# Linear attention with a gated MoE: queries projected with the tokens moving, the row maximum taken across partitions, three quads of keys unpaired

## The chip, the core and the metric

The kernel runs on one core of a Trainium2 chip. The metric is the device time of one launch in microseconds (us), the median of three runs. Engines are named as in the profile: PE is TensorE (matmuls; PEld its weight loads), DVE is VectorE, ACT is ScalarE, POOL is GpSimd, SP is SyncE, whose queue issues the DMAs.

## The reference

Eight batches, eight heads, 576 tokens, head dimension 64. Queries and keys go through the same feature map with 128 features: a projection, minus the largest absolute value of each row, then exp of it and of its negative.

```
def phi(x):
    proj = np.einsum('bhsd,df->bhsf', x, w_phi)
    proj = proj - np.max(np.abs(proj), axis=-1, keepdims=True)
    return np.concatenate([np.exp(proj), np.exp(-proj)], axis=-1)
q_p, k_p = (phi(q), phi(k))
kv = np.einsum('bhsf,bhsd->bhfd', k_p, v)
z = np.sum(k_p, axis=2)
num = np.einsum('bhsf,bhfd->bhsd', q_p, kv)
den = np.einsum('bhsf,bhf->bhs', q_p, z)[..., None] + 1e-06
attn = num / den
h = np.maximum(x @ w_in, 0.0)              # x: attn, heads joined; 512 -> 1024
conv_out = sum over k of conv_w[k] * h shifted by k - 1 tokens
out = (h * sigmoid(conv_out)) @ w_out      # 1024 -> 512
```

## The kernel before

**Precision.** Most products are made of three float32r matmuls: each operand is split into a rounded part (`hi`) and the rest (`lo`), and hi*hi, hi*lo and lo*hi are summed in PSUM. Some products of the first two quads are plain float32, in one matmul instruction, which the trace shows as two matmul records.

**Tiling.** A "quad" is (b, qd): one batch and four of its heads, 16 quads in all. A quad has five groups g of tokens: g = 0 has one tile of 128 columns, g = 1 to 4 have n = 2 tiles. A tile holds 128 tokens of two heads (64 + 64 partitions), so a quad has nine tiles and the kernel 144 for queries and 144 for keys.

**Keys** (`k_process`): load, split on GpSimd (`load_split`, L172 to L183), project (L199 to L201, three matmuls of 256 columns a tile, tokens as the stationary operand, so that tokens come out on partitions), maximum and subtraction on VectorE (L204, L206), two exps on ScalarE (L236, L237), then the key-value products L251 and L255. From the sixth group on (`j < 5` at L260) these products are not issued by the key's own step but handed over in `kvgen`, and the queries' step puts them between its own matmuls ("paired").

**Queries** (`q_process`): load, split on GpSimd, project in the same way (L196 in float32 for the first two quads, L199 to L201 after), maximum and subtraction on VectorE (`qm`, `qs`), then PE transposes (L320, two a tile, into `tp`), because the following products need features on partitions. ScalarE takes the exps from `tp` (L326), splits them with VectorE (`qh`, `ql`), and PE makes numerator and denominator `nm` (L348 float32, L356 split).

**Normalisation and MoE.** `x_process` takes reciprocals of the denominators, spreads them by DMA over `rr`, and makes `xh`, `xl` for one head pair and half (c) of the tokens. `h_part(n)`, n = 2b + c, makes `hp` (L429), ScalarE applies relu (L436), GpSimd and VectorE do the convolution (L452, L457), ScalarE the sigmoid, VectorE the gate (L465) and the split `gl`, and `o_part(n)` the output product `op` (L488). The 16 pieces of the two MoE weights arrive as float64 words and are rounded on VectorE (L96 to L103), ScalarE and GpSimd (`w_t`), while the attention of the first quads runs.

**What sets the order.** A planner (the loop at L558) keeps up to 13 steps of `chains` active, advances each step when its planned time has come (`wait`, `pe`) and its keys in `ready` are set (`until`), and lets attention and MoE take turns on PE. The framework's scheduler then orders the instructions of each engine with its own timing, within the planner's priorities; on the chip each engine runs its list strictly in that order. PSUM tiles `qp`, `kp`, `tp`, `nm` share four buffers (tag `g`), the MoE's `hp` and `op` two others.

## Time and profile before

| | |
|---|---|
| median of three runs | 826.61 us (825.32 to 826.67) |
| profiled execution, its own time | 825.6 us |
| its span, first to last instruction | 823.5 us |
| mean granted PE clock | 0.989 |
| ScalarE busy | 569.5 us (69%) |
| first output product `op` L488 starts | 191.8 us into the span |
| DMA, share of 16 engines | 20.1% |

A group's row gives line, engine, operation, output and inputs, their shapes and the count, then its busy time, the mean of one in ns, and the engine's idle time just before it with what ended it. Matmuls overlap in the records, so what a matmul costs a busy PE is not its duration but the distance from its start to the next matmul's start, which a timeline shows.

### The profile page before, as it was taken

To read this page: it belongs to the slowest core of one execution; us is meant where nothing else is said; L and a number is where in the kernel's file an instruction comes from. 1 tells how busy PE (TensorE), PEld (TensorE's weight loads), DVE (VectorE), ACT (ScalarE), POOL (GpSimd) and SP (SyncE) were. 2 spreads that over 40 slices of the span, in tenths; PEclk is the share of its full clock that TensorE was granted. 3 is DMA by queue.
4 is the path that set the end of the run, shared out by engine and by line. 5 is a ranking of instruction groups with operands and counts; after the bars stand their busy time and mean duration, and the time that the engine had idled before them with its cause. 6 is when DMAs were issued, how large, how long until landed. Compare 5 with 4: busy or idle time off the path is not lost.

```text
span 823.5 us, 17817 instructions
## 1 busy us (share of the span) xinstructions
PE 788.0 (96%) x6350; PEld 772.5 (94%) x6350; DVE 645.6 (78%) x1390; ACT 569.5 (69%) x1228; POOL 307.6 (37%) x467
## 2 busy tenths in 40 slices
PE   7778779999999999999999999999999999999998
PEld 6767678999999999999999999999999999999998
DVE  4879999799987769787779878788697878766551
ACT  4598777797788867687586857678576867644332
POOL 4757765444443424414233333424334131111110
PEclk9799989999999999999999999999999999999999
DMA  6544421211211302121121211112021100000001
GB/s 187 157 134 135 135 66 47 67 41 44 70 56 44 93 18 71 27 82 50 46 61 43 69 34 60 47 50 82 15 77 29 56 12 19 13 30 30 23 23 44
DMA packets 56328, 49.18 MB, mean 60 GB/s; under 512 B 15024, under 2 KB 54192, under 8 KB 56240
## 3 DMA queue, kind: packets, MB, share of 16 engines
q1 hardware_dynamic: 56240, 48.05, 20.1%
q8 instruction: 51, 0.84, 0.4%
q14 instruction: 37, 0.30, 0.1%
HBM read 38.13 MB, written 9.44 MB: 58 GB/s over the span
## 4 chain that ended last, share of the span: by engine, by line
PE 74%; DVE 10%; ACT 7%; issue 4%; DMA 3%; POOL 1%; SPq 1%; DVEq 0%; ACTq 0%; POOLq 0%
PE op L488 22%; PE hp L429 21%; PE kv L255 8%; PE nm L356 8%; PE tp L320 3%; PE kp L199 2%; PE nm L348 2%; PE kp L200 2%; PE kp L201 2%; PE qp L199 1%; PE qp L200 1%; PE qp L201 1%; DMA w_r<-in_w_in_dram 1%; PE kv L251 1%; DVE qm L204 1%
## 5 line engine op out<-in xcount | busy, mean ns | idle before, releaser
L457 DVE SCALAR_TENSOR_TENSOR c<-h,cw,c 128x287 f32<-128x287 f32 (+1 forms) x256 | 138.7, 554 | 49.4 <-POOL c L452 47.5
L452 POOL TENSOR_SCALAR c<-h,cw 128x288 f32<-128x288 f32 x128 | 75.0, 588 | 243.6 <-ACT h L436 184.3
L255 PE MATMUL kv<-v,ke 128*128 128x65 f32 x1024 | 159.4, 255 | 1.4 <-ACT ke L236 1.2
L255 PEld LDWEIGHTS kv<-v,ke 128*128 128x128 f32 x1024 | 153.5, 193 | 4.8 <-ACT ke L236 1.8
L429 PE MATMUL hp<-xh,win_hi 128*128 128x290 f32 x512 | 153.2, 300 | 0.6 <-ACT os L493 0.6
L429 PE MATMUL hp<-xl,win_hi 128*128 128x290 f32 x512 | 152.7, 298 | 0.2 <-DVE xl L65 0.2
L488 PE MATMUL op<-gh,wout_hi 128*128 128x288 f32 x512 | 152.2, 298 | 0.0
L429 PE MATMUL hp<-xh,win_lo 128*128 128x290 f32 x512 | 151.9, 297 | 0.0
L488 PE MATMUL op<-gl,wout_hi 128*128 128x288 f32 x512 | 151.4, 296 | 0.0
L488 PE MATMUL op<-gh,wout_lo 128*128 128x288 f32 x512 | 150.9, 295 | 0.0
L436 ACT ACTIVATE h<-hp 128x290 f32<-128x290 f32 x128 | 52.2, 414 | 71.7 <-PE hp L429 71.2
L429 PEld LDWEIGHTS hp<-xh,win_hi 128*128 128x128 f32 x512 | 96.7, 190 | 1.5 <-ACT os L493 1.4
L62 POOL TENSOR_SCALAR kxh<-kr 128x256 fp32r<-128x256 f32 (+1 forms) x80 | 43.8, 547 | 144.1 <-PE kp L200 134.6
L429 PEld LDWEIGHTS hp<-xl,win_hi 128*128 128x128 f32 x512 | 97.0, 189 | 0.6 <-DVE xl L65 0.6
L429 PEld LDWEIGHTS hp<-xh,win_lo 128*128 128x128 f32 x512 | 97.1, 190 | 0.0
L488 PEld LDWEIGHTS op<-gh,wout_lo 128*128 128x128 f32 x512 | 96.4, 188 | 0.0
L488 PEld LDWEIGHTS op<-gl,wout_hi 128*128 128x128 f32 x512 | 96.2, 188 | 0.0
L488 PEld LDWEIGHTS op<-gh,wout_hi 128*128 128x128 f32 x512 | 96.1, 188 | 0.0
L65 DVE TENSOR_TENSOR ql<-qe,qh 128x512 fp32r<-128x512 f32 x112 | 79.9, 732 | 9.9 <-ACT qh L60 9.5
L236 ACT ACTIVATE ke<-ks 128x512 f32<-128x512 f32 (+1 forms) x80 | 46.9, 586 | 39.1 <-DVE ks L206 36.5
L326 ACT ACTIVATE qe<-tp 128x512 f32<-128x512 f32 x112 | 61.2, 595 | 12.2 <-PE tp L320 10.4
L356 PE MATMUL nm<-ql,kvh 128*65 128x256 f32 x224 | 68.4, 308 | 0.3 <-DVE ql L65 0.2
(84 smaller groups left out, 1989.5 us busy)
## 6 DMA issues: line engine op xcount, KB each, us to landing
v<-in_vt_dram SPq DMA_DIRECT2D x80, 130.0 KB
out_dram<-os SPq DMA_DIRECT2D x64, 144.0 KB
qr<-in_qT_dram SPq DMA_DIRECT2D x64, 128.0 KB
kr<-in_kT_dram SPq DMA_DIRECT2D x64, 128.0 KB
w_r<-in_w_in_dram SPq DMA_DIRECT2D x8, 512.0 KB
...
rr<-rc SPq DMA_DIRECT2D x128, 2.2 KB
...
```

Source lines behind the costliest of these rows:

```text
L62: nc.gpsimd.tensor_scalar(out=hi, in0=src, scalar1=1.0, scalar2=0.0, op0=ALU.mult, op1=ALU.add)
L65: eng_lo.tensor_tensor(out=lo, in0=src, in1=hi.bitcast(F32), op=ALU.subtract)
L199: nc.tensor.matmul(out=o, lhsT=his, rhs=wbd_hi, start=True, stop=False)
L236: nc.scalar.activation(out=e[:, 0], in_=pr, func=AF.Exp)
L255: ins = nc.tensor.matmul(out=kp[i][:, s, p0 : p0 + VW], lhsT=lhsT, rhs=v[:, (2 * t + i) * VW : (2 * t + i + 1) * VW], start=False, stop=(g ...
L326: nc.scalar.activation(out=e, in_=tp.rearrange("p i t s -> p i (t s)"), func=AF.Exp, scale=1.0 - 2.0 * s)
L356: ins = after(ins, lambda: nc.tensor.matmul(out=ps[:, i, o : o + w], lhsT=w_, rhs=x_, start=(k == 0), stop=(k == 5)))
L429: nc.tensor.matmul(out=ps, lhsT=w_, rhs=x_, start=(k == 0), stop=(k == 11))
L436: nc.scalar.activation(out=hs, in_=ps, func=AF.Relu)
L452: nc.gpsimd.tensor_scalar(out=cv, in0=hs[:, o : o + TC], scalar1=cw[:, f, 1:2], scalar2=0.0, op0=ALU.mult, op1=ALU.add)
L457: nc.vector.scalar_tensor_tensor(out=cv[:, lo:hi], in0=hs[:, o + j - 1 + lo : o + j - 1 + hi], scalar=cw[:, f, j : j + 1], in1=cv[:, lo:hi ...
L488: nc.tensor.matmul(out=ps, lhsT=w_, rhs=x_, start=(k == 0), stop=(k == 23))
```

## The change

**Queries' projection.** The weights become the stationary operand and the tokens move, so that features come out on partitions at once and no transposes are needed. One tile `qp` of 128 x 512 (n = 2) holds both heads of both token tiles. Matmul L337 takes the rounded weights `wq_hi` (in both halves of the partitions) and `x`, whose lower 64 partitions hold the rounded query and whose upper 64 the rest; L338 adds the rest of the weights. For the first two quads one float32 matmul of 64 rows (L340) stands in their place.

**The maximum.** It must now be taken across partitions. A VectorE reduction with transposition (L346) gives, for each block of 32 partitions, the maxima of 32 features; three copies (L349) bring the four blocks to the same partitions, a second reduction (L351) joins them, a cast and a subtraction (L353, L354) split the result. GpSimd multiplies it with a 32 x 32 identity into the upper half of `x` (L357), and a last matmul L366, with weights of -1 (`wq_m`), subtracts the maximum from all features in PSUM. The exps read `qp` itself.

**Loads and splits.** Each query group is loaded twice (both halves of the partitions, two DMAs of 64 partitions; once for the first two quads), and GpSimd rounds 128 x 512 (L199) and subtracts 64 x 512 (L200).

**Order.** The products of the first three quads' keys are issued by the key's own step (`PAIR_FROM`), and the first batch's steps enter the planner in strict order: keys then queries of quad 0, keys then queries of quad 1, then the keys of the next quad. The planner's times for the query steps change with the code.

```diff
+PAIR_FROM = 3
...
+        if kind == "q":
+            f32 = 2 * b + qd < NQ_F32
+            raw = sb.tile([P, 2, n * P], F32, name=f"qr{b}_{qd}_{g}", tag="qr", bufs=2)
+            for h in range(1 if f32 else 2):
+                nc.sync.dma_start(out=raw[D * h : D * h + D, :, :],
+                                  in_=src[b, qd, :, c0 : c0 + n * P].rearrange("(i d) s -> d i s", d=D))
+            x = sb.tile([P, 2, n * P], F32R, name=f"qx{b}_{qd}_{g}", tag="qx", bufs=2)
...
+            nc.gpsimd.tensor_scalar(out=x, in0=raw, scalar1=1.0, scalar2=0.0, op0=ALU.mult, op1=ALU.add)
+            nc.gpsimd.tensor_tensor(out=x[D:P], in0=raw[D:P], in1=x[D:P].bitcast(F32), op=ALU.subtract)
...
-        if j < 5:
+        if j < 5 * PAIR_FROM:
...
+        tp = pg.tile([P, 2, n, P], F32, name=f"qp{b}_{qd}_{g}", tag="g", bufs=4)
...
+            nc.tensor.matmul(out=tpf, lhsT=wq_hi, rhs=xf, start=True, stop=False, skip_group_check=True)
+            nc.tensor.matmul(out=tpf, lhsT=wq_lo, rhs=xf, start=False, stop=False, skip_group_check=True)
...
+            nc.vector.tensor_reduce(out=mt[:, 2, 0:c], in_=tpf.rearrange("p (c f) -> p c f", f=32), axis=AX, op=ALU.max,
+                                    apply_absolute_value=True, apply_transpose=True)
+            for a in (0, 1, 3):
+                nc.vector.tensor_copy(out=mt[D : D + 32, a, 0:c], in_=mt[32 * a : 32 * a + 32, 2, 0:c])
...
+            nc.vector.tensor_reduce(out=m[D : D + 32, 0:c], in_=mt[D : D + 32, :, 0:c].rearrange("p a c -> p c a"), axis=AX, op=ALU.max)
...
+            nc.gpsimd.tensor_tensor(out=xf[D:P, :].rearrange("p (c t) -> p c t", t=32),
...
-                nc.tensor.transpose(out=tp[:, i, t, :], in_=pr[:, 2 * t + i, :], identity=idn)
+            nc.tensor.matmul(out=tpf, lhsT=wq_m[r, :], rhs=xf[r, :], start=False, stop=True, skip_group_check=True)
...
-        paired = j + 5 < 5 * NQ * B
+        paired = 5 * PAIR_FROM <= j + 5 < 5 * NQ * B
...
-    chains = [(0, 0, g, "k") for g in range(5)]
-    for u in range(NQ * B):
+    chains = [(0, u, g, k) for u in range(2) for k in "kq" for g in range(5)] + [(1, 0, g, "k") for g in range(5)]
+    for u in range(2, NQ * B):
```

PE's list in the middle of the program, batch 4, in which a name such as `qp4_0_3` is the tile of batch 4, quad 0, group 3; before, the projection of group 3 with the transposes of group 2 among it:

```order
L199 MATMUL kp4_1_2_5558<-wbd_hi_72,kxh4_1_2_5441 128x256
L199 MATMUL qp4_0_3_5572<-wbd_hi_72,qxh4_0_3_5449 128x256
L320 MATMUL tp4_0_2_5517<-idn_76,qs4_0_2_5437 128x128
L200 MATMUL qp4_0_3_5572<-wbd_lo_73,qxh4_0_3_5449 128x256
L255 MATMUL kv4_1_0_5489<-v4_1_1_5184,ke4_1_1_5425 128x65
L200 MATMUL kp4_1_2_5558<-wbd_lo_73,kxh4_1_2_5441 128x256
L320 MATMUL tp4_0_2_5517<-idn_76,qs4_0_2_5437 128x128
L201 MATMUL qp4_0_3_5572<-wbd_hi_72,qxl4_0_3_5450 128x256
```

The same place on PE now:

```order
L475 MATMUL hp5_0_4650<-xh2_3_1_4377,win_lo3_110 128x290
L337 MATMUL qp4_0_3_5594<-qx4_0_3_5506,wq_hi_76 128x512
L338 MATMUL qp4_0_3_5594<-qx4_0_3_5506,wq_lo_77 128x512
L402 MATMUL nm4_0_1_5608<-qh4_0_1_5531,kvh4_0_0_5398 65x256
L276 MATMUL kv4_1_0_5541<-v4_1_1_5234,ke4_1_1_5478 128x65
L402 MATMUL nm4_0_1_5608<-ql4_0_1_5532,kvh4_0_0_5398 65x256
L276 MATMUL kv4_1_0_5541<-v4_1_1_5234,ke4_1_1_5478 128x65
L402 MATMUL nm4_0_1_5608<-qh4_0_1_5531,kvl4_0_0_5399 65x256
L402 MATMUL nm4_0_1_5608<-qh4_0_1_5531,kvh4_0_0_5398 65x256
L366 MATMUL qp4_0_2_5481<-qx4_0_2_5239,wq_m_78 128x512
```

The transposes are gone, the projection is two wide matmuls, and the matmul that subtracts the maximum (L366) stands far behind them: the one of `qp4_0_3` has 58 other matmuls between L338 and itself.

VectorE's list at that place, before:

```order
L204 TENSOR_REDUCE qm4_0_3_5579<-qp4_0_3_5572 128x4
L206 TENSOR_TENSOR ks4_1_2_5567<-kp4_1_2_5558,km4_1_2_5565 128x512
L65 TENSOR_TENSOR ql4_0_2_5523<-qe4_0_2_0_5524,qh4_0_2_5522 128x512
L206 TENSOR_TENSOR qs4_0_3_5581<-qp4_0_3_5572,qm4_0_3_5579 128x512
L65 TENSOR_TENSOR ql4_0_2_5523<-qe4_0_2_1_5528,qh4_0_2_5522 128x512
```

and now:

```order
L346 TENSOR_REDUCE qmt4_0_3_5597<-qp4_0_3_5594 128x16
L349 COPY qmt4_0_3_5597<-qmt4_0_3_5597 32x16 x3
L351 TENSOR_REDUCE qm4_0_3_5602<-qmt4_0_3_5597 32x16
L503 SCALAR_TENSOR_TENSOR c5_5189<-h5_0_4663,cw_92,c5_5189 128x288
L353 CAST qmp4_0_3_5604<-qm4_0_3_5602 32x16
L67 TENSOR_TENSOR ql4_0_2_5571<-qe4_0_2_0_5572,qh4_0_2_5570 128x512
L503 SCALAR_TENSOR_TENSOR c5_5189<-h5_0_4663,cw_92,c5_5189 128x287
L354 TENSOR_TENSOR qmp4_0_3_5604<-qm4_0_3_5602,qmp4_0_3_5604 32x16
```

One reduction and one subtraction of 128 x 512 became one reduction of that size and six small operations, with three other instructions between them.

VectorE's list at the end of the start, where the first convolution instruction `c0` stands (in its 197th row before and its 221st now; `w13`, `w15` are pieces of the MoE weights). Before:

```order
L103 SCALAR_TENSOR_TENSOR w15_t_897<-w15_t_897,w15_r_895 128x512
L65 TENSOR_TENSOR xl0_3_1_1534<-xf0_3_1_1530,xh0_3_1_1533 128x290
L65 TENSOR_TENSOR ql1_0_4_1494<-qe1_0_4_0_1495,qh1_0_4_1493 128x512
L204 TENSOR_REDUCE km2_0_0_1541<-kp2_0_0_1537 128x2
L65 TENSOR_TENSOR ql1_0_4_1494<-qe1_0_4_1_1499,qh1_0_4_1493 128x512
L204 TENSOR_REDUCE qm1_1_1_1555<-qp1_1_1_1548 128x4
L206 TENSOR_TENSOR ks2_0_0_1543<-kp2_0_0_1537,km2_0_0_1541 128x256
L405 STREAM_SHUFFLE xf1_0_0_1998<-rr_78 128x290
L405 STREAM_SHUFFLE xf1_0_1_2143<-rr_78 128x290
L206 TENSOR_TENSOR qs1_1_1_1557<-qp1_1_1_1548,qm1_1_1_1555 128x512
L204 TENSOR_REDUCE qm1_1_2_1574<-qp1_1_2_1567 128x4
L457 SCALAR_TENSOR_TENSOR c0_1877<-h0_0_1611,cw_82,c0_1877 128x287
```

and now:

```order
L346 TENSOR_REDUCE qmt1_1_0_1461<-qp1_1_0_1458 128x8
L349 COPY qmt1_0_4_1432<-qmt1_0_4_1432 32x16 x3
L349 COPY qmt1_1_0_1461<-qmt1_1_0_1461 32x8 x3
L114 TENSOR_SCALAR w13_t_916<-w13_r_914 128x512
L351 TENSOR_REDUCE qm1_0_4_1437<-qmt1_0_4_1432 32x16
L116 SCALAR_TENSOR_TENSOR w13_t_916<-w13_r_914,w13_t_916 128x512
L351 TENSOR_REDUCE qm1_1_0_1466<-qmt1_1_0_1461 32x8
L67 TENSOR_TENSOR ql1_0_2_1381<-qe1_0_2_0_1382,qh1_0_2_1380 128x512
L119 SCALAR_TENSOR_TENSOR w13_t_916<-w13_t_916,w13_r_914 128x512
L503 SCALAR_TENSOR_TENSOR c0_1932<-h0_0_1667,cw_92,c0_1932 128x287
```

The first convolution stands two pieces of the weights earlier (piece 13 instead of 15 just ahead of it), and the attention of batch 1 is less far along when it is reached (`ql1_0_2` instead of `ql1_0_4`).

More of the change, by code (lines that the diff above doesn't have):

```diff
@@ L78 @@
     split(wbd_f, wbd_hi, wbd_lo, nc.vector, nc.vector)
-    idn = load_const(ident, [P, P], "idn")
+    wq_hi = cp.tile([P, F], F32R, name="wq_hi")
+    wq_lo = cp.tile([P, F], F32R, name="wq_lo")
+    wq_m = cp.tile([P, F], F32R, name="wq_m")
+    for i in range(2):
+        r = slice(D * i, D * i + D)
+        nc.vector.tensor_copy(out=wq_hi[r, :], in_=wbd_hi[r, i * F : (i + 1) * F].bitcast(F32))
+    eye = cp.tile([P, 32], F32, name="eye")
+    for p in (D, D + 32):
+        nc.sync.dma_start(out=eye[p : p + 32, :], in_=ident[p : p + 32, p : p + 32])
     rr = cp.tile([P, S], F32, name="rr")
     nc.gpsimd.memset(rr, 0.0)
+    nc.gpsimd.tensor_copy(out=wq_m, in_=rr[:, 0:F])
+    nc.gpsimd.tensor_copy(out=wq_lo, in_=rr[:, 0:F])
+    nc.vector.tensor_copy(out=wq_lo[0:D, :], in_=wbd_lo[0:D, 0:F].bitcast(F32))
+    nc.gpsimd.tensor_scalar(out=wq_m[D:P, :], in0=rr[D:P, 0:F], scalar1=-1.0, scalar2=0.0, op0=ALU.add, op1=ALU.add)
     bias_e = cp.tile([P, 1], F32, name="bias_e")
@@ L173, in load_split @@
         c0, n = group_columns(g)
[L174 to L177 removed]
+        if kind == "q":
[5 more added lines that the diff above has]
+            x = sb.tile([P, 2, n * P], F32R, name=f"qx{b}_{qd}_{g}", tag="qx", bufs=2)
+            if f32:
+                return n, x, raw
+            nc.gpsimd.tensor_scalar(out=x, in0=raw, scalar1=1.0, scalar2=0.0, op0=ALU.mult, op1=ALU.add)
+            nc.gpsimd.tensor_tensor(out=x[D:P], in0=raw[D:P], in1=x[D:P].bitcast(F32), op=ALU.subtract)
+            return n, x, None
         raw = sb.tile([P, n * P], F32, name=f"{kind}r{b}_{qd}_{g}", tag=kind + "r", bufs=2)
@@ L194, in project @@
             his = hi[:, t * P : (t + 1) * P]
-            if lo is None:
-                nc.tensor.matmul(out=o, lhsT=his, rhs=wbd_f, start=True, stop=True)
-                continue
             los = lo[:, t * P : (t + 1) * P]
@@ L306, in q_process @@
         yield until(back("qp", 2))
-        n, hi, lo = load_split(qT, b, qd, g, "q")
+        n, x, raw = load_split(qT, b, qd, g, "q")
         yield wait(3000)
@@ L310, in q_process @@
         set_ready(("qp", *divmod(j, 5)))
-        pr = project(n, hi, lo, b, qd, g, "q")
-        yield pe(330 * n)
-        yield wait(1700)
+        w = n * 2 * P
+        tp = pg.tile([P, 2, n, P], F32, name=f"qp{b}_{qd}_{g}", tag="g", bufs=4)
+        tpf = tp.rearrange("p i t s -> p (i t s)")
+        xf = x.rearrange("p i s -> p (i s)")
+        if raw is None:
+            nc.tensor.matmul(out=tpf, lhsT=wq_hi, rhs=xf, start=True, stop=False, skip_group_check=True)
+            nc.tensor.matmul(out=tpf, lhsT=wq_lo, rhs=xf, start=False, stop=False, skip_group_check=True)
+        else:
+            nc.tensor.matmul(out=tpf, lhsT=wbd_f[0:D, 0:F], rhs=raw.rearrange("p i s -> p (i s)")[0:D], start=True, stop=False,
+                             skip_group_check=True)
@@ L314, in q_process @@
+        yield pe(230 * n)
+        yield wait(2500)
         yield until(back("num", 2))
         set_ready(("tp", *divmod(j, 5)))
-        tp = pg.tile([P, 2, n, P], F32, name=f"tp{b}_{qd}_{g}", tag="g", bufs=4)
-        for t in range(n):
-            for i in range(2):
-                nc.tensor.transpose(out=tp[:, i, t, :], in_=pr[:, 2 * t + i, :], identity=idn)
+        r = slice(0, P) if raw is None else slice(D, P)
+        with tc.high_priority():
+            nc.tensor.matmul(out=tpf, lhsT=wq_m[r, :], rhs=xf[r, :], start=False, stop=True, skip_group_check=True)
```

18 lines of the change are left out of this document (12 added, 6 removed).

## The prediction

> **What bounds the kernel now.** I read the page first, then the table of windows cut at the first MoE result, then timelines of PE for what a matmul costs there.
>
> ```profile
> span 823.5 us, 17817 instructions
> PE 788.0 (96%) x6350; PEld 772.5 (94%) x6350; DVE 645.6 (78%) x1390; ACT 569.5 (69%) x1228; POOL 307.6 (37%) x467
> ...
> PE   7778779999999999999999999999999999999998
> ...
> DVE  4879999799987769787779878788697878766551
> ```
>
> The profiled execution took 825.6 us, of which 823.5 are its span; the sum below is made against 825.6, and the median of the runs, 826.61, is 1.0 above it. A slice is 20.6 us: PE is full from the seventh on (some 124 us); in most of the six before, VectorE is the fuller one. The first relu, in the timeline of ScalarE, marks the end of this start:
>
> ```profile
> 128.14 0.72 ACT L436 ACTIVATE h<-hp 128x290 f32<-128x290 f32 x2
> ```
>
> The table of windows, cut there (columns: window, its length, then busy time and count of PE, PEld, DVE, ACT, POOL, clock, DMA):
>
> ```profile
> 0.00:128.10 128.10, 98.88 (x685) 88.22 (x686) 107.99 (x197) 92.97 (x195) 83.42 (x101) 0.93 0.45 133
> 128.10:823.50 695.40, 689.10 (x5667) 684.26 (x5665) 537.58 (x1194) 476.56 (x1034) 224.18 (x367) 1.00 0.16 46
> ```
>
> After 128.1 us PE is idle for 6.3 us of 695.4: there a PE matmul saved is time saved, one for one. Before it PE is idle for 29 us and VectorE, at 108 of 128 us, is what comes nearest to a bound: there PE's savings are worth nothing by themselves, and VectorE's list counts.
>
> **What a matmul costs a full PE.** Two pieces of PE's timeline, start times first:
>
> ```profile
> 418.79 0.30 PE L429 MATMUL hp<-xl,win_hi 128*128 128x290 f32 x1
> 418.93 0.30 PE L429 MATMUL hp<-xh,win_lo 128*128 128x290 f32 x1
> ...
> 419.91 0.28 PE L199 MATMUL qp<-wbd_hi,qxh 128*128 128x256 f32 x1
> 420.03 0.28 PE L200 MATMUL qp<-wbd_lo,qxh 128*128 128x256 f32 x1
> 420.15 0.28 PE L201 MATMUL qp<-wbd_hi,qxl 128*128 128x256 f32 x1
> 420.26 0.29 PE L429 MATMUL hp<-xl,win_hi 128*128 128x290 f32 x1
> ```
>
> ```profile
> 48.24 0.60 PE L348 MATMUL nm<-qh,kvh 128*65 128x256 f32 x2
> 48.67 0.56 PE L255 MATMUL kv<-v,ke 128*128 128x65 f32 x4
> 49.06 0.60 PE L348 MATMUL nm<-qh,kvh 128*65 128x256 f32 x2
> 49.50 0.60 PE L320 MATMUL tp<-idn,qs 128*128 128x128 f32 x4
> 49.93 0.33 PE L255 MATMUL kv<-v,ke 128*128 128x65 f32 x2
> ```
>
> From start to start a float32r matmul of 256 columns takes 0.117 us (three in 0.35) and one of 290 about 0.14: it goes by columns, so 512 columns, which no row shows, should take 0.234. Bounds: 0.21 (less, if part of the 0.117 is fixed) to 0.26. A transpose takes 0.108 (four in 0.43). A key-value instruction is two records, so 0.39 us for two instructions, 0.195 each.
>
> **PE, the whole kernel.** Out go 288 transposes, 288 x 0.108 = 31.1 us. The split projection was 3 x 126 tiles of 256 columns and becomes two passes over the same columns: 126 x 0.117 = 14.7 us less. The new maximum matmul passes over all 144 tiles: 144 x 0.117 = 16.8 us more. The float32 projections of the first two quads pass over as many columns as before. Sum: **-29.0 us**; with the bounds of the 512 columns (176 such matmuls, -0.024 to +0.026 each) -33 to -24.
>
> **How much of that lies ahead of the first relu.** By the order of PE's list up to the last matmul of the first `hp`, there stand 15 key projections fewer (1.8 us), 16 key-value instructions fewer (3.1), 24 split `nm` fewer (2.8), the split projection of queries in 14 instead of 36 matmuls' worth of 256 columns (2.6), 25 such of the new maximum (-2.9) and 56 transposes fewer (6.0): 13.4 us. So the rest of PE's list, which is what counts after that point, is shorter by 29.0 - 13.4 = **15.6 us**.
>
> **The start, by VectorE's list.** What stands ahead of its first convolution instruction is priced by its groups by form (busy, mean ns, idle before):
>
> ```profile
> L65 DVE TENSOR_TENSOR ql<-qe,qh 128x512 fp32r<-128x512 f32 x112 | 79.9, 732 | 9.9 <-ACT qh L60 9.5
> L457 DVE SCALAR_TENSOR_TENSOR c<-h,cw,c 128x288 f32<-128x288 f32 x128 | 69.5, 549 | 17.9 <-POOL c L452 17.1
> L206 DVE TENSOR_TENSOR qs<-qp,qm 128x512 f32<-128x512 f32 x64 | 43.0, 678 | 0.1
> L204 DVE TENSOR_REDUCE qm<-qp 128x4 f32<-128x512 f32 x64 | 43.0, 678 | 0.8 <-PE qp L201 0.8
> L405 DVE STREAM_SHUFFLE xf<-rr 128x290 f32<-128x290 f32 x64 | 29.0, 484 | 0.4 <-issue 0.4
> L103 DVE SCALAR_TENSOR_TENSOR w_t<-w_t,w_r 128x512 f32<-128x512 int32 x16 | 14.8, 922 | 0.0
> L100 DVE SCALAR_TENSOR_TENSOR w_t<-w_r,w_t 128x512 int32<-128x512 int32 x16 | 12.4, 777 | 0.0
> L98 DVE TENSOR_SCALAR w_t<-w_r 128x512 int32<-128x512 int32 x16 | 9.6, 602 | 6.5 <-ACT w_t L97 6.5
> L96 DVE TENSOR_SCALAR w_t<-w_r 128x512 int32<-128x512 int32 x16 | 8.6, 539 | 2.0 <-DMA w_r<-in_w_in_dram 1.0 <-POOL wout_lo L65 0.8
> L393 DVE RECIPROCAL rc<-den 72x16 f32<-72x16 f32 x32 | 7.7, 240 | 0.1
> L204 DVE TENSOR_REDUCE qm<-qp 128x2 f32<-128x256 f32 x16 | 6.6, 413 | 0.7 <-PE qp L201 0.7
> L96 DVE TENSOR_SCALAR cw<-cw_raw 128x24 int32<-128x24 int32 x1 | 0.2, 176 | 0.0
> ```
>
> Out: 27 query reductions and subtractions of 512 (18.3) and 8 of 256 (3.3), two key operations of each size (2.2), five `ql` (3.7), two weight pieces of 0.54 + 0.60 + 0.78 + 0.92 (5.7), two shuffles, a reciprocal and its addition (1.5): 34.7 us. In: 12 transposing reductions of 512 and 4 of 256, 48 copies, 16 second reductions, 28 casts and subtractions of the maxima, three copies of constants. No row shows a transposing reduction. The nearest is the plain one of the same shape, 0.68; its bounds are 0.54, the lowest row of 512 elements, and 1.36, two passes. For the small ones the nearest rows are 0.176 (128x24) and 0.240 (72x16); I take 0.17 for copies, casts and subtractions and 0.24 for the second reduction, and bound them by half, since records of neighbours may overlap. In: 9.8 + 8.2 + 3.8 + 4.8 + 0.6 = 27.2 us. Net **-7.5 us**; -16 with the small ones at half, +2 with the transposing reduction at two passes. I take the start as that much shorter, 120.6 us instead of 128.1.
>
> [...]
>
> The unpaired products of quads 1 and 2 stand in this start too. In the float32 quads pairing hides little that I can see (0.195 us beside the 0.43 of an `nm`, in the second timeline), so I price them at nothing, bounded by 64 more weight loads of two records that nothing covers,
>
> ```profile
> L255 PEld LDWEIGHTS kv<-v,ke 128*128 128x128 f32 x1024 | 153.5, 193 | 4.8 <-ACT ke L236 1.8
> ```
>
> at most 64 x (0.386 - 0.195) = 12 us, which PE's 29 idle us of the start cover.
>
> **GpSimd.** Its rows:
>
> ```profile
> L65 POOL TENSOR_TENSOR qxl<-qr,qxh 128x256 fp32r<-128x256 f32 x56 | 47.4, 854 | 1.7
> L62 POOL TENSOR_SCALAR qxh<-qr 128x256 fp32r<-128x256 f32 x56 | 26.4, 473 | 62.3 <-PE qp L200 62.1
> L105 POOL TENSOR_TENSOR w_t<-w_t 128x512 f32<-128x512 f32 x16 | 22.0, 1373 | 10.0 <-DVE w_t L103 7.4 <-DVE den L392 2.6
> ```
>
> A group of two tiles took 0.47 + 0.85 = 1.3 us. Now it is a rounding of 512 (0.47 to 0.95, I take 0.7) and two two-input operations of 512 (1.4 each): 3.5 us. The 70 split groups and 10 float32 ones make some 150 us more, 458 of 805 us, 57%. Nothing waits on that total; its cover is that PE has other work. VectorE adds 80 x about 0.45 = 35 us, 85% of the new span.
>
> **The new chain.** From L338 to L366 the chain is now the transposing reduction 0.68, three copies 0.51, reduction 0.24, cast and subtraction 0.34 and GpSimd's product 1.4, with the matmul's own end (0.28) 3.45 us, plus what stands between them in the lists: in the place shown `ql` and two convolution steps, 0.73 + 2 x 0.55, so 5.3. L366 has 58 matmuls ahead of it there, at 0.117 to 0.195 some 8 us. The old chain's last link shows how often such an order is missed:
>
> ```profile
> L320 PE MATMUL tp<-idn,qs 128*128 128x128 f32 x288 | 58.6, 277 | 4.4 <-DVE ks L206 4.0 <-DVE qs L206 0.2
> ```
>
> 4.4 us in all. Behind a waiting L366 all of PE's list is queued, and so ScalarE's exps. I price its waits at **+2 us**, with bounds of 0 and 12 (64 such matmuls after the start, 0.2 us each). The query loads double from 80 to 150 DMAs on SP's queue; they wait for GpSimd's last reading of the raw tile,
>
> ```profile
> SPq L179 <- POOL qxl L65: 55.9, 39, 4.0
> ```
>
> which is now later by 2 us a group; a wait there costs nothing as long as PE has the MoE's matmuls in front of it.
>
> **Sum.** 825.6 - 7.5 - 15.6 + 2 = **804.5 us**.
>
> **The rivals.** *The start shrinks with PE.* If PE's work and not VectorE's list sets the length of the start, it gets shorter by the 13.4 us taken out ahead of the relu: 825.6 - 13.4 - 15.6 = 796.6. For it speaks that the strict order unties the first quads; against it VectorE's 108 of 128 us.
>
> *VectorE and GpSimd get into each other's way.* Their rows show it already: in the answer on the tile `w_t` (min/median/max)
>
> ```profile
> L103 DVE SCALAR_TENSOR_TENSOR w_t<-w_t,w_r x16: 674/750/1762, 21.9 to 124.8; 128x512 f32<-128x512 int32 x16
> ```
>
> the same operation takes up to 1 us more while GpSimd computes weights. With 150 us more of GpSimd, VectorE's 85% would come near 90%, small waits appear on PE, and 12 us of them give 814.5. [...]
>
> *The maximum comes too late.* PE stands at L366 for the chain through VectorE and GpSimd. 64 of them follow the start; the gain of 23.1 us is gone when each waits 0.36 us on average. If half of them wait 0.9 us, that is 29 us and 831.5. It decides where chain and queues pass the 8 us of cover, that is, where the queues take over 4.5 us beside the chain's 3.45. Against it speak the 4.4 us of the old link.
>
> *The start does not shrink.* GpSimd's share of the weights comes later behind its query work, the relu stays at 128 us or later by some 6: 825.6 + 6 - 15.6 + 8 = 824.
>
> **Chances.** Forecast 0.5, short start 0.2, contention 0.15, no change 0.06, too late 0.09. The range reaches over the short start, with 512 columns at their lowest bound, to contention with a start that gains little: 790 to 820. A difference under 0.2%, about 1.7 us, cannot be told from none: faster 0.86, same 0.05, slower 0.09.
>
> **What would show it.** Right: the first relu near 120 us, PE idle for less than 9 us after it, 0.234 us from an L337 to the next matmul, a transposing reduction of 0.68, L366 waiting a few us in all. Wrong: a relu at 115 or before (the short start), L366 high in the list of waits (too late), two-input rows of VectorE well over their means here (contention), or 512 columns at another price.

## The result, and the profile after

The changed kernel takes **949.62 us** (median of four runs, 949.2 to 951.72) against 826.59 beside it: a ratio of 1.150, with an interval of 1.148 to 1.152. The forecast was 804.5, its range 790 to 820: a gain of 21 us was forecast and a loss of 123 was measured. The page of the profile after, with busy time, slices and the chain that ended last:

```profile
span 947.7 us, 17471 instructions
PE 823.3 (87%) x5888; PEld 766.4 (81%) x5888; DVE 812.0 (86%) x1793; ACT 572.4 (60%) x1228; POOL 447.6 (47%) x550
...
PE   8978668896798888799898889897988979999998
...
DVE  7898999999799899889997998898889879876652
...
DVE 49%; PE 25%; ACT 8%; issue 7%; POOL 5%; DMA 3%; SPq 1%; DVEq 0%; POOLq 0%; ACTq 0%
```

The chain of the kernel before, from its page:

```profile
PE 74%; DVE 10%; ACT 7%; issue 4%; DMA 3%; POOL 1%; SPq 1%; DVEq 0%; ACTq 0%; POOLq 0%
```

VectorE is busy for 7 tenths or more in each of the first 36 of 40 slices, mostly 8 or 9, and is now the largest part of the chain (49%, where PE had 74%); PE, which was full from the seventh slice on before, now has gaps up to the 33rd. VectorE's busy time rose by 166 us (645.6 to 812.0); the forecast had 35. The first relu comes at 131.5 us (before 128.1, forecast near 120). The table of windows, cut there (columns as in the prediction):

```profile
0.00:131.50 131.50, 102.83 (x536) 78.14 (x536) 116.09 (x241) 77.72 (x165) 83.96 (x101) 0.84 0.41 118
131.50:947.70 816.20, 720.45 (x5353) 688.26 (x5352) 695.94 (x1553) 494.66 (x1064) 363.60 (x450) 0.95 0.18 51
```

So the start cost 3.4 us and the rest 120.8. In the rest PE is idle for 816.2 - 720.45 = 95.8 us, against 6.3 before. PE's busy time grew by 31 us although it ran 314 matmuls fewer; its granted clock is 0.95 there, against 1.00.

Where VectorE's 166 us come from, by its groups by form (columns: busy us, mean ns, idle before; "gl" is the low half of the gate's product):

```profile
L67 DVE TENSOR_TENSOR ql<-qe,qh 128x512 fp32r<-128x512 f32 x112 | 94.4, 850 | 6.6 <-ACT qh L62 5.6
L503 DVE SCALAR_TENSOR_TENSOR c<-h,cw,c 128x288 f32<-128x288 f32 x128 | 82.5, 648 | 16.9 <-POOL c L498 15.4
L511 DVE TENSOR_TENSOR c<-c,h 128x288 f32<-128x288 f32 x128 | 75.6, 657 | 11.7 <-ACT c L507 11.5
L67 DVE TENSOR_TENSOR gl<-c,gh 128x288 fp32r<-128x288 f32 x128 | 61.4, 522 | 17.9 <-ACT gh L62 16.9
L346 DVE TRANSPOSE_TENSOR_REDUCE qmt<-qp 128x16 f32<-128x512 f32 x64 | 45.1, 705 | 2.3 <-PE qp L338 1.2 <-PE qp L340 0.7
L349 DVE COPY qmt<-qmt 32x16 f32<-32x16 f32 x192 | 44.3, 231 | 3.6
L353 DVE CAST qmp<-qm 32x16 fp32r<-32x16 f32 x64 | 16.5, 258 | 2.3
L351 DVE TENSOR_REDUCE qm<-qmt 32x16 f32<-32x64 f32 x64 | 16.3, 254 | 1.9
L354 DVE TENSOR_TENSOR qmp<-qm,qmp 32x16 fp32r<-32x16 f32 x64 | 12.3, 192 | 2.0
L349 DVE COPY qmt<-qmt 32x8 f32<-32x8 f32 x48 | 11.6, 241 | 1.0
```

The reader is to see two things. The new small instructions (all rows of 32 partitions, with 10.4 us of three smaller groups that are not shown) take 111 us, where 0.17 and 0.24 apiece would have made 87. And instructions that the change does not touch are longer: `ql` 850 ns against 732, the convolution's step 648 against 549, the gate's product `c<-c,h` 657 against 502 and `gl` 522 against 461. The last two rows of before, which the prediction does not show:

```profile
L465 DVE TENSOR_TENSOR c<-c,h 128x288 f32<-128x288 f32 x128 | 56.0, 502 | 7.7 <-ACT c L461 7.7
L65 DVE TENSOR_TENSOR gl<-c,gh 128x288 fp32r<-128x288 f32 x128 | 51.4, 461 | 14.3 <-ACT gh L60 14.1
```

By their busy times (79.9, 69.5, 56.0 and 51.4 before) these four are 57 us. The transposing reductions, 52 us, stand in place of some 99 us of reductions and subtractions; the remaining 45 us are other older instructions that last longer, and less overlap of neighbours.

What stands behind the longer ones can be seen in one piece of the timeline, VectorE first, then GpSimd in the same 9 us (start, us, how many):

```profile
290.65 0.53 DVE L349 COPY qmt<-qmt 32x16 f32<-32x16 f32 x3
291.21 0.17 DVE L353 CAST qmp<-qm 32x16 fp32r<-32x16 f32 x1
...
291.97 0.17 DVE L354 TENSOR_TENSOR qmp<-qm,qmp 32x16 fp32r<-32x16 f32 x1
292.38 7.07 DVE L511 TENSOR_TENSOR c<-c,h 128x288 f32<-128x288 f32 x8 [0.25 <-ACT c L507]
299.38 0.68 DVE L225 TENSOR_REDUCE km<-kp 128x4 f32<-128x512 f32 x1
```

```profile
292.20 2.27 POOL L357 TENSOR_TENSOR qx<-qmp,eye 64x512 fp32r<-64x512 f32 x2 [6.90 <-DVE qmp L354]
294.55 0.71 POOL L199 TENSOR_SCALAR qx<-qr 128x512 fp32r<-128x512 f32 x1
...
296.28 1.37 POOL L200 TENSOR_TENSOR qx<-qr,qx 64x512 fp32r<-64x512 f32 x1
...
298.20 0.94 POOL L67 TENSOR_TENSOR kxl<-kr,kxh 128x256 fp32r<-128x256 f32 x1
```

Eight products of the gate take 0.88 us each while GpSimd works almost without a gap; their mean was 0.50 before. Not all of VectorE's instructions got longer: those that read the projected keys in PSUM, L225 and L227 of 128 x 512, kept their 680 and 683 ns (681 and 681 before).

The small instructions are held up too, but in another way (the view of a tile: shortest, median and longest in ns, then first and last start):

```profile
L349 DVE COPY qmt<-qmt x240: 161/167/1233, 5.9 to 821.4; 32x16 f32<-32x16 f32 x96, 32x8 f32<-32x8 f32 x24
L353 DVE CAST qmp<-qm x80: 152/166/1136, 7.6 to 824.9; 32x16 fp32r<-32x16 f32 x64, 32x8 fp32r<-32x8 f32 x16
```

Their median is the 0.17 of the forecast. A few last much longer, such as the cast here, beside GpSimd's product:

```profile
591.31 0.91 DVE L353 CAST qmp<-qm 32x16 fp32r<-32x16 f32 x1
590.97 1.23 POOL L357 TENSOR_TENSOR qx<-qmp,eye 64x512 fp32r<-64x512 f32 x1 [8.55 <-DVE qmp L354]
```

The cast ends 0.02 us after the product that was under way when it began. In the whole trace 47 of the 480 last more than 0.32 us, copies, casts and subtractions but no reduction, and each of them ends 0.02 to 0.03 us after a GpSimd instruction that was running when it began. These 47 take 31.6 us instead of some 8, which is nearly all of the difference between 111 and 87.

The waits that the forecast feared most are there, but small (engine, line, waited for: us in all, times, longest):

```profile
PE qp L366 <- POOL qx L357: 33.1, 29, 3.2
PE qp L337 <- POOL qx L200: 12.0, 12, 2.5
PE kp L220 <- DVE ks L227: 10.1, 4, 6.5
```

33.1 us at L366 is more than the 12 of the bound, and less than a third of the loss.

### The profile page after: what moved, and what is told of

Read it like the earlier page. It is cut to its first block, busy times and chain, and to the rows that moved or that the text cites. A ratio compares the mean times of both kernels' runs of the same rounds, so it can differ in the third digit from the quotient of the medians.

```text
span 947.7 us, 17471 instructions
## 1 busy us (share of the span) xinstructions
PE 823.3 (87%) x5888; PEld 766.4 (81%) x5888; DVE 812.0 (86%) x1793; ACT 572.4 (60%) x1228; POOL 447.6 (47%) x550
## 4 chain that ended last, share of the span: by engine, by line
DVE 49%; PE 25%; ACT 8%; issue 7%; POOL 5%; DMA 3%; SPq 1%; DVEq 0%; POOLq 0%; ACTq 0%
DVE c L503 9%; PE hp L475 8%; PE op L534 8%; DVE c L511 5%; DVE ql L67 5%; DVE qmt L349 4%; DVE qmt L346 3%; DVE gl L67 3%; DVE km L225 3%; DVE ks L227 2%; PE kv L276 2%; PE nm L402 2%; DVE xf L452 2%; DVE xf L451 2%; DVE w_t L116 2%
## 5 line engine op out<-in xcount | busy, mean ns | idle before, releaser
L357 POOL TENSOR_TENSOR qx<-qmp,eye 64x512 fp32r<-64x512 f32 (+1 forms) x80 | 85.1, 1067 | 228.8 <-DVE qmp L354 213.4
L503 DVE SCALAR_TENSOR_TENSOR c<-h,cw,c 128x287 f32<-128x287 f32 (+1 forms) x256 | 161.9, 646 | 32.9 <-POOL c L498 29.9
L475 PE MATMUL hp<-xh,win_hi 128*128 128x290 f32 x512 | 157.8, 310 | 10.5 <-ACT xh L62 4.1
L276 PE MATMUL kv<-v,ke 128*128 128x65 f32 x1024 | 164.3, 263 | 2.1 <-ACT ke L257 2.1
L276 PEld LDWEIGHTS kv<-v,ke 128*128 128x128 f32 x1024 | 157.9, 201 | 7.2 <-ACT ke L257 3.1
L475 PE MATMUL hp<-xh,win_lo 128*128 128x290 f32 x512 | 155.5, 304 | 0.0
L498 POOL TENSOR_SCALAR c<-h,cw 128x288 f32<-128x288 f32 x128 | 79.4, 624 | 129.3 <-ACT h L482 101.1
L67 DVE TENSOR_TENSOR ql<-qe,qh 128x512 fp32r<-128x512 f32 x112 | 94.4, 850 | 6.6 <-ACT qh L62 5.6
L200 POOL TENSOR_TENSOR qx<-qr,qx 64x512 fp32r<-64x512 f32 (+1 forms) x70 | 90.4, 1294 | 5.0
L372 ACT ACTIVATE qe<-qp 128x512 f32<-128x512 f32 x112 | 62.3, 594 | 43.4 <-DVE ql L67 23.8
## 6 DMA issues: line engine op xcount, KB each, us to landing
qr<-in_qT_dram SPq DMA_DIRECT2D x120, 128.0 KB
kr<-in_kT_dram SPq DMA_DIRECT2D x64, 128.0 KB
```

Of the source, the lines that this page charges most:

```text
L67: eng_lo.tensor_tensor(out=lo, in0=src, in1=hi.bitcast(F32), op=ALU.subtract)
L200: nc.gpsimd.tensor_tensor(out=x[D:P], in0=raw[D:P], in1=x[D:P].bitcast(F32), op=ALU.subtract)
L276: ins = nc.tensor.matmul(out=kp[i][:, s, p0 : p0 + VW], lhsT=lhsT, rhs=v[:, (2 * t + i) * VW : (2 * t + i + 1) * VW], start=False, stop=(g ...
L357: nc.gpsimd.tensor_tensor(out=xf[D:P, :].rearrange("p (c t) -> p c t", t=32), in0=mp[D:P, 0:c].bitcast(F32).unsqueeze(2).broadcast_to([D, ...
L372: nc.scalar.activation(out=e, in_=tp.rearrange("p i t s -> p i (t s)"), func=AF.Exp, scale=1.0 - 2.0 * s)
L475: nc.tensor.matmul(out=ps, lhsT=w_, rhs=x_, start=(k == 0), stop=(k == 11))
```

## The experiments

Four theories are named in what was expected. **V**: VectorE has become the bound, by its own new instructions and by older ones that last longer beside GpSimd's. **L**: the maximum's chain is too slow and PE stands at L366. **O**: the strict order and the unpaired products cost it. **Q**, formed after small_ops: a small instruction is dear because it reads or writes at another quadrant (32 partitions) than its neighbours. Times are medians; each interval is that of the ratio to the kernel before on the same chip.

**Is it the order?** In the changed kernel the old order (order_back), in the kernel before the new one (order_alone):

```diff
-PAIR_FROM = 3
+PAIR_FROM = 1
...
-    chains = [(0, u, g, k) for u in range(2) for k in "kq" for g in range(5)] + [(1, 0, g, "k") for g in range(5)]
-    for u in range(2, NQ * B):
+    chains = [(0, 0, g, "k") for g in range(5)]
+    for u in range(NQ * B):
...
-            if u + 1 < NQ * B and u > 0:
+            if u + 1 < NQ * B:
```

> The changed kernel with its new query projection, but with the old order: PAIR_FROM = 1 (only the first quad's products unpaired) and the old list of steps. Theory V (VectorE became the bound: its small operations for the maximum, and its two-input operations held up by GpSimd's added work): nothing of this is touched, 930 to 960 us, VectorE busy again 800 to 820 us. Theory L (PE waits in order at the late matmul L366): 920 to 960. Theory O (the new order and the unpaired products cost the time): back to 840 or less.

> The kernel before with only the order of the change: PAIR_FROM = 3 and the strict list of steps; queries projected as before. Theory V and theory L: 820 to 835 us, since neither VectorE nor the chain changes. Theory O: most of the 123 us of the change, over 880.

Order_back 946.67 us, 1.146 (1.133 to 1.158): not told apart from the changed kernel. Order_alone 843.58, 1.021 (1.018 to 1.024): on the kernel before the order costs 17 us by itself, which lies between what V and L had said (835 at most) and O (over 880). Its first relu comes at 109.3 us, 19 earlier than before, and the rest is 36 us longer. O falls as the main cause.

**Is it the chain?** No_wait lets L366 read the lower 64 rows, whose weights are zero, so that nothing waits for the chain and the maximum is left out of the split quads:

```diff
-        r = slice(0, P) if raw is None else slice(D, P)
+        r = slice(0, D) if raw is None else slice(D, P)
```

> The changed kernel with L366 of the split quads reading the lower 64 rows of x with zero weights instead of GpSimd's product, so that PE, ScalarE and all that follows no longer wait for the chain through VectorE and GpSimd, whose instructions all stay (left out: the subtraction of the maximum in quads 2 to 15). Theory L (PE's waits for that chain cost the time): most of the 123 us come back, 860 or less. Theory V (VectorE and its contention with GpSimd are the bound): 920 to 950, VectorE busy still over 790.

961.43 us, 1.163 (1.159 to 1.168): no gain at all, so the 33.1 us at L366 were no cost by themselves. L falls as the main cause. V had said 920 to 950; why this kernel is 12 us slower than the changed one was not settled.

**Is it VectorE's own instructions?** No_copies takes the three copies and the second reduction out (the maximum is then that of one block of 32 rows); copies_scalar gives the copies to ScalarE:

```diff
-            for a in (0, 1, 3):
-                nc.vector.tensor_copy(out=mt[D : D + 32, a, 0:c], in_=mt[32 * a : 32 * a + 32, 2, 0:c])
-            m = sb.tile([P, 16], F32, name=f"qm{b}_{qd}_{g}", tag="qm", bufs=2)
-            nc.vector.tensor_reduce(out=m[D : D + 32, 0:c], in_=mt[D : D + 32, :, 0:c].rearrange("p a c -> p c a"), axis=AX, op=ALU.max)
+            m = mt[:, 2, :]
```

```diff
-                nc.vector.tensor_copy(out=mt[D : D + 32, a, 0:c], in_=mt[32 * a : 32 * a + 32, 2, 0:c])
+                nc.scalar.activation(out=mt[D : D + 32, a, 0:c], in_=mt[32 * a : 32 * a + 32, 2, 0:c], func=AF.Copy)
```

> The changed kernel without the three copies and the second reduction of a query group: the maximum is that of one block of 32 features alone (left out: the other 96 features). VectorE loses 240 copies and 80 reductions, 75 us of its busy time by their rows. Theory V: 860 to 890 us, VectorE busy under 750. Theory L: the chain to L366 gets shorter by 0.75 us of some 5, PE's waits at L366 (33 us) halve at most: 920 to 940. Theory O: no change, 945 to 955.

> The changed kernel with the three copies of each query group on ScalarE (240 of them, some 0.2 us each, ScalarE busy 572 to some 620). The chain to L366 stays as long or gets longer, VectorE loses 56 us. Theory V: 890 to 920 us. Theory L: 945 to 970.

No_copies 900.29 us, 1.089 (1.084 to 1.095), 10 us above what V had said; copies_scalar 916.48, 1.109 (1.105 to 1.113), as V had said. The copies cost 33 us on VectorE even where the chain keeps them: V holds.

**The same instructions alone.** Small_ops adds to the kernel before, in the program behind each query projection, three copies, a reduction, a cast and a subtraction of the same shapes, on tiles that nobody reads:

```diff
+        for a in (0, 1, 3):
+            nc.vector.tensor_copy(out=mt[D : D + 32, a, 0:c], in_=mt[32 * a : 32 * a + 32, 2, 0:c])
+        m = sb.tile([P, 16], F32, name=f"xm{b}_{qd}_{g}", tag="xm", bufs=2)
+        nc.vector.tensor_reduce(out=m[D : D + 32, 0:c], in_=mt[D : D + 32, :, 0:c].rearrange("p a c -> p c a"), axis=AX, op=ALU.max)
+        mp = sb.tile([P, 16], F32R, name=f"xmp{b}_{qd}_{g}", tag="xmp", bufs=2)
+        nc.vector.tensor_copy(out=mp[D : D + 32, 0:c], in_=m[D : D + 32, 0:c])
+        nc.vector.tensor_tensor(out=mp[D + 32 : P, 0:c], in0=m[D : D + 32, 0:c], in1=mp[D : D + 32, 0:c].bitcast(F32),
+                                op=ALU.subtract)
```

> The kernel before with the six small VectorE operations of each query group added (three copies, a reduction, a cast, a subtraction, on scratch tiles that nobody reads; 480 in all, 110 us in the changed kernel), on no chain. Theory V: VectorE busy 730 to 760, the time 845 to 880. Theory L: 826 to 832, since no engine waits for them.

928.76 us, 1.124 (1.119 to 1.128): 102 us for 480 instructions on no chain, more than theory V had given them (845 to 880). Since they wait for nothing, they also run early: the last copy starts at 383.9 us, against 821.4 in the changed kernel. So the 102 us are the price of crowded instructions, and do not carry over to the changed kernel as they stand. The page of small_ops:

```profile
PE 825.5 (89%) x6350; PEld 799.1 (86%) x6350; DVE 768.8 (83%) x1870; ACT 574.0 (62%) x1228; POOL 303.9 (33%) x468
```

VectorE rose by 123 us (645.6 to 768.8), 0.26 us for each of them. VectorE's timeline there shows how a small instruction stands among the others:

```profile
296.62 0.53 DVE L317 COPY mt<-mt 32x16 f32<-32x16 f32 x3
297.18 0.17 DVE L321 CAST xmp<-xm 32x16 fp32r<-32x16 f32 x1
297.38 0.69 DVE L209 TENSOR_TENSOR qs<-qp,qm 128x512 f32<-128x512 f32 x1
297.98 0.32 DVE L64 CAST kvh<-kvf 128x260 fp32r<-128x260 f32 x1
```

The cast starts 0.56 us after the copies, which take 0.53, and the `qs` 0.20 after the cast, which takes 0.17: each begins when the one before has ended. Between `qs` and `kvh`, both of 128 partitions, the second begins 0.60 us after a first that takes 0.69: they overlap by 0.09. So it is in the whole trace: from the end of an instruction to the start of the next, where VectorE did not wait between them, the median is +0.03 us between a small and a large one, and -0.08 between two large ones. The cast reads and writes the same partitions, 64 to 95, so it is not a move between partitions that keeps it apart. The half-price bound of the prediction rested on such overlap.

**Small_level** has the same instructions, all in partitions 0 to 31; **small_late** has those of small_ops in the split quads only. Small_level against small_ops:

```diff
-            nc.vector.tensor_copy(out=mt[D : D + 32, a, 0:c], in_=mt[32 * a : 32 * a + 32, 2, 0:c])
+            nc.vector.tensor_copy(out=mt[0:32, a, 0:c], in_=mt[0:32, 2, 0:c])
...
-        nc.vector.tensor_copy(out=mp[D : D + 32, 0:c], in_=m[D : D + 32, 0:c])
+        nc.vector.tensor_copy(out=mp[0:32, 0:c], in_=m[0:32, 0:c])
```

> The kernel of small_ops (before, with 480 small VectorE instructions that nobody reads), with all of them in partitions 0 to 31, so that none reads or writes at another quadrant than its neighbours. If the price of a small instruction comes from the change of quadrant, their mean falls from 0.25 to 0.18 us or less and the time from 929 to 860 to 900 us. If it is the price of any instruction in VectorE's list, the means stay at 0.22 to 0.27 and the time at 910 to 935.

> The kernel of small_ops with the six small instructions only in the groups of the split quads (the first two quads, 10 of 80 groups, without). If VectorE's added time costs wherever it stands: 7/8 of the 102 us, 905 to 920 us. If it costs because the start gets longer (the first relu of small_ops comes at 171 us, against 128): 840 to 880.

Small_level: 855.67 us, 1.036 (1.033 to 1.039), 73 us less than small_ops, 4 us better than Q had said. Its page and a piece of VectorE's timeline:

```profile
PE 797.6 (93%) x6350; PEld 778.8 (91%) x6350; DVE 706.5 (83%) x1870; ACT 573.4 (67%) x1228; POOL 344.6 (40%) x468
```

```profile
291.09 0.30 DVE L317 COPY mt<-mt 32x16 f32<-32x16 f32 x3
291.32 0.15 DVE L321 CAST xmp<-xm 32x16 fp32r<-32x16 f32 x1
291.40 0.28 DVE L64 CAST kvh<-kvf 128x260 fp32r<-128x260 f32 x1
```

The cast now begins 0.23 us after the first of the three copies instead of 0.56, and the next instruction 0.08 us after the cast, whose record lasts 0.15. By the same count over the trace the median between a small and a large one is now -0.07 to -0.08 us, as between two large ones. VectorE's busy time fell by 62 us, 0.13 for each of the 480. One sign in the expectation failed: the mean of the records hardly fell (a copy 226 ns against 264), since a record shows how long an instruction lasts and not how much of it lies beside the one before; and in both kernels some of the small ones stand until a GpSimd instruction ends (69 and 67 of 480 last over 0.32 us). What in VectorE keeps such instructions apart, and at which partitions it begins, is shown by no run: small ones that write partitions 64 to 127 were compared with small ones at 0 to 31.

Small_late: 914.12 us, 1.106 (1.104 to 1.108), 88 of the 102 us for seven eighths of the instructions. The cost goes with their number; but the first relu came late here too (173.1 us, small_ops 171.1). VectorE runs 436 instructions ahead of it, against 197 in the kernel before, so more than half of the 420 stand in the start, and this run doesn't tell the start from the rest.

**Q in the changed kernel itself.** After_level puts the six instructions of each group in partitions 0 to 31 and gives GpSimd's product a constant tile of zeros:

```diff
-                nc.vector.tensor_copy(out=mt[D : D + 32, a, 0:c], in_=mt[32 * a : 32 * a + 32, 2, 0:c])
+                nc.vector.tensor_copy(out=mt[0:32, a, 0:c], in_=mt[0:32, 2, 0:c])
...
-                                    in0=mp[D:P, 0:c].bitcast(F32).unsqueeze(2).broadcast_to([D, c, 32]),
+                                    in0=mpc[D:P, 0:c].unsqueeze(2).broadcast_to([D, c, 32]),
```

> The changed kernel with the same six small VectorE instructions a group, all in partitions 0 to 31; GpSimd's product takes its maxima from a constant tile of zeros, so the output leaves the maximum out. Theory Q (a small instruction is dear because it reads or writes at another quadrant than its neighbours, so that it cannot overlap them): as between small_ops and small_level, VectorE's busy time falls by about 60 us and the time by 60 to 80, to 870 to 890 us. Rival (in the changed kernel the small instructions cost by their number): 930 to 960.

885.47 us, 1.072 (1.069 to 1.074): 64 us of the 123 come back. VectorE went from 812.0 to 751.3 with the same 1793 instructions, about as much as from small_ops to small_level. But the constant tile changes a second thing: GpSimd's product no longer waits for VectorE's maxima (213 us of GpSimd's waiting in the changed kernel) and runs at other moments. The gate's product fell from 657 to 496 ns, 20 us in all, while the mean of the small casts rose from 258 to 335. So the 64 us are the quadrants and this shift together; the clean comparison of quadrants is small_ops with small_level.

**GpSimd beside VectorE.** Gpsimd_load gives the kernel before 208 two-input GpSimd subtractions that nobody reads; no_rest takes the remainder of the split queries, L200, out of the changed kernel (it is left out of the result):

```diff
+        for i in range(2 * n - 1):
+            nc.gpsimd.tensor_tensor(out=load[D:P, :], in0=wbd_f[D:P, :], in1=wbd_f[D:P, :], op=ALU.subtract)
```

```diff
-            nc.gpsimd.tensor_tensor(out=x[D:P], in0=raw[D:P], in1=x[D:P].bitcast(F32), op=ALU.subtract)
```

> The kernel before with 208 GpSimd subtractions of 64x256 added that nobody reads (some 150 us of GpSimd time, about what the change adds). If GpSimd's work holds up VectorE's two-input operations (part of theory V): the means of ql, of the convolution steps and of the gate rise (732 to over 800 ns, 555 to over 600), VectorE busy rises by 40 to 90 us from 646, and the time to 835 to 870 us. If not: means as before and 825 to 832 us.

> The changed kernel without GpSimd's subtraction L200 (left out: the rest of the split queries; the rounded query stands in both halves). GpSimd loses 90 us of two-input work, VectorE no instruction; beside these L200 its operations ran 53 us longer in the changed kernel than at their usual length. Contention as part of theory V: VectorE busy falls by 30 to 60 us without an instruction less and the time to 890 to 925. Without contention: VectorE busy 800 or more, time 935 to 950.

Gpsimd_load 881.62 us, 1.067 (1.063 to 1.071), 12 us above its interval, with VectorE at 702.5 for the same 1390 instructions, 57 us more. Most of that load ran in the first 16 slices, where GpSimd was nearly full, so part of the time may be GpSimd's own work coming late. No_rest has no such doubt: 898.7 us, 1.087 (1.081 to 1.094), 51 us less than the changed kernel (its first relu comes at 121.3 us, 10 earlier). Its page, and two of VectorE's groups:

```profile
PE 811.7 (91%) x5888; PEld 758.3 (85%) x5888; DVE 749.5 (84%) x1793; ACT 573.1 (64%) x1228; POOL 361.5 (40%) x480
```

```profile
L67 DVE TENSOR_TENSOR ql<-qe,qh 128x512 fp32r<-128x512 f32 x112 | 83.4, 750 | 15.6 <-ACT qh L62 14.6
...
L510 DVE TENSOR_TENSOR c<-c,h 128x288 f32<-128x288 f32 x128 | 53.1, 480 | 11.9 <-ACT c L506 11.7
```

VectorE's busy time fell by 62 us without one VectorE instruction less; `ql` is back from 850 to 750 ns and the gate's product from 657 to 480, while the reduction of the keys, which reads PSUM, stays at 680. L200 has two inputs; GpSimd's instructions of one input were not taken out in any run.

**What is left of the forecast's gain?** Both_out takes away what no_copies and no_rest take away; all_out also the cast and the subtraction on VectorE and, in the split quads, GpSimd's product, so that of the new VectorE work only the transposing reduction stays. Both were also run with the old order. The core of all_out, against the changed kernel:

```diff
-            mp = sb.tile([P, 16], F32R, name=f"qmp{b}_{qd}_{g}", tag="qmp", bufs=2)
-            nc.vector.tensor_copy(out=mp[D : D + 32, 0:c], in_=m[D : D + 32, 0:c])
-            nc.vector.tensor_tensor(out=mp[D + 32 : P, 0:c], in0=m[D : D + 32, 0:c], in1=mp[D : D + 32, 0:c].bitcast(F32),
-                                    op=ALU.subtract)
...
+            if raw is not None:
```

> The changed kernel with both suspected loads away at once: without the three copies and the second reduction on VectorE, and without GpSimd's remainder of the split queries (the maximum is then that of one block of 32 rows, and the split queries have no low half). Theory V (VectorE is the bound, by its own small instructions and by the longer ones beside GpSimd): the two gains of 49 and 51 us add up nearly, 835 to 870 us, VectorE's busy time near 670. If both only removed the same idle time of TensorE: 885 to 900.

> The kernel of both_out with the old order (pairing from the second quad, the list of chains of the kernel before). Theory V with the order as an extra cost of some 17 us where VectorE is not the bound (as in order_alone): 15 to 20 us below both_out, 815 to 850 us; with VectorE's and GpSimd's loads gone the gain of TensorE's shorter list should then show, toward 805. Rival (the new TensorE form with its chain costs something by itself): as both_out, or 845 and more.

> The kernel of both_out without the cast and the subtraction of the maxima on VectorE and, for the split quads, without GpSimd's product (the maximum is left out altogether; of VectorE's new work the transposing reduction alone remains, which nobody waits for). Theory V: VectorE falls from 691 to about 620 us and TensorE's shorter list shows: 800 to 835 us. Rival (TensorE's new form or the new order costs by itself): 845 to 875, as both_out.

> The kernel of all_out with the old order (pairing from the second quad, the old list of chains). Theory V: 10 to 17 us below all_out, 790 to 820 us: the forecast's 804.5 would be what the change is worth without its load on VectorE and GpSimd. Rival (TensorE's new form costs by itself): 830 or more.

| kernel | us | ratio (interval) | VectorE busy | first relu at |
|---|---|---|---|---|
| both_out | 875.51 | 1.061 (1.056 to 1.066) | 691.4 | 134.5 |
| both_out_order | 862.03 | 1.043 (1.038 to 1.048) | 680.2 | 142.4 |
| all_out | 823.50 | 0.997 (0.992 to 1.003) | 614.4 | 138.5 |
| all_out_order | 824.21 | 0.999 (0.995 to 1.003) | 615.2 | 128.0 |

Both_out and both_out_order missed their intervals by 6 and 12 us on the upper side: the two gains of 49 and 51 us don't add up, together they are 74. All_out came within its range, all_out_order 4 us above. With nearly all the new load gone, 126 us are gone; what remains is a kernel equal to the one before, not the forecast's 804.5. The windows of all_out, cut at its first relu, show why (its profiled execution has a span of 828.3):

```profile
0.00:138.50 138.50, 120.78 (x603) 93.84 (x603) 103.14 (x177) 90.57 (x189) 84.83 (x103) 0.89 0.46 130
138.50:828.30 689.80, 669.00 (x5285) 653.41 (x5285) 511.22 (x1137) 485.69 (x1040) 205.86 (x309) 1.00 0.20 57
```

After the relu PE's busy time is 669.0 against 689.1, 20 us less. Some 8 of these (an estimate, 68 matmuls at 0.12) are matmuls that stand ahead of the relu here and behind it in the changed kernel. But PE is idle there for 20.8 us instead of 6.3, and the start is 10 us longer although VectorE, 103 of 138.5 us, no longer fills it. Over the whole span PE is busy for 789.8 us, as before (788.0), since its busy time in the start rose by 22 us. In all_out_order the start is as before, PE's busy time after it 674.6 us, and its idle time there 21 us again.

**A complete version.** Spread keeps the whole computation, with the old order, the copies and the cast on ScalarE and the subtraction on GpSimd:

```diff
-            nc.vector.tensor_copy(out=mp[D : D + 32, 0:c], in_=m[D : D + 32, 0:c])
-            nc.vector.tensor_tensor(out=mp[D + 32 : P, 0:c], in0=m[D : D + 32, 0:c], in1=mp[D : D + 32, 0:c].bitcast(F32),
+            nc.scalar.activation(out=mp[D : D + 32, 0:c], in_=m[D : D + 32, 0:c], func=AF.Copy)
+            nc.gpsimd.tensor_tensor(out=mp[D + 32 : P, 0:c], in0=m[D : D + 32, 0:c], in1=mp[D : D + 32, 0:c].bitcast(F32),
```

> The changed kernel, complete, with the old order, the three copies and the cast of the maxima on ScalarE and the subtraction on GpSimd, so that VectorE has the transposing and the second reduction alone. Theory V: below copies_scalar (916), 880 to 905 us, and still slower than the kernel before, because GpSimd's two-input instructions remain beside VectorE's.

900.89 us, 1.093 (1.089 to 1.096), as V had it: 49 us better than the changed kernel, and slower than the one before. No version that was run beats the kernel before.

## Why the prediction was wrong, step by step

- **The step that failed** is the one under GpSimd: "Nothing waits on that total; its cover is that PE has other work. VectorE adds 80 x about 0.45 = 35 us, 85% of the new span." VectorE's share came out at 86%, but of a span 145 us longer than forecast: 812.0 us of work and not some 681 (645.6 + 35). PE did not cover it: VectorE is 49% of the chain that ended last, and the term that was put at nothing is worth 126 us (949.6 to all_out's 823.5). Two mechanisms make it up. The small instructions at other quadrants don't overlap their neighbours (between a small and a large one a median of +0.03 us from the end of the first to the start of the next, in small_ops and in the changed kernel alike; -0.07 to -0.08 in small_level): 62 us of VectorE's time from small_ops to small_level, and in the changed kernel 64 us of time by after_level, where GpSimd's product moved too. And VectorE's instructions are held up by GpSimd's: 51 us of time and 62 us of VectorE's by no_rest, which takes out one two-input instruction in each of the 70 split groups. The two were measured one at a time and needn't add up.
- **The rival of contention** had the mechanism, and was priced by its symptom, "12 us of them give 814.5", and not by its own row, a `w_t` step of up to 1 us more; the sign named for it, two-input rows well over their means, is what the groups after show (`ql` 850 ns against 732, the gate's product 657 against 502). Without L200 `ql`, which has two inputs in SBUF, took 750 ns instead of 850; why GpSimd's work lengthens it was not shown.
- **The small instructions' price.** 0.17 was taken for copies, casts and subtractions, and that is the median record. The means are 0.19 to 0.27, because one in ten stands until a GpSimd instruction ends. What the forecast missed besides is that they don't overlap their neighbours, so that each also takes away the overlap that a neighbour had: 0.26 us apiece in small_ops. The nearest rows were those of instructions that start at partition 0, which is what mattered here: 0.13 us apiece in small_level, where the small ones start there too.
- **The start, -7.5 us.** It went +3.4. That VectorE's list alone sets its length is refuted by all_out and all_out_order, whose starts are 138.5 and 128.0 us with the same 103 us of VectorE's work in them. What does set it was not settled; the granted clock of the start is 0.84 after and 0.89 in all_out, against 0.93.
- **PE's list, -15.6 us after the relu.** The size was about right: PE's busy time there fell by 20 us in all_out and by 14.5 in all_out_order, of which some 8 are matmuls that moved ahead of the relu. But "there a PE matmul saved is time saved, one for one" was not: the idle time after the relu grew by 14.5 us even without the load. In that trace no single wait explains it; the largest is PE's for ScalarE's `num`, 5.1 us in all.
- **The order** was priced at nothing for the unpaired products, and the strict order only as something that helps the start. On the kernel before it does shorten the start, by 19 us, but costs 36 behind it, 17 in all; in the changed kernel that is hidden.
- **The waits at L366**, +2 us with a bound of 12: 33.1 us measured, yet taking them away gained nothing. That the time was VectorE's in any case is argued and not shown; VectorE is busy for 807.9 us in no_wait.
- **Right** were the transposing reduction (0.68 taken, 0.705 measured), 512 columns on PE (0.234 taken; 0.227 to 0.239 from an L337 of 512 columns to the next matmul in 28 of 56 in the trace after, longer in the others), the two-input GpSimd instructions and GpSimd's total (458 forecast, 447.6 measured).
- **Open**: by the two tables of windows the rest of the changed kernel is 126 us longer than that of all_out, of which 75 are PE's idle time (95.8 against 20.8) and 51 its busy time, with 68 matmuls more behind the cut and a granted clock of 0.95 instead of 1.00. How much of the 51 is the clock, and what lowered it, was not told apart.
